# Front of a gated two-branch attention kernel: two loads of weights put first, and a longer slot in the planner of the products

## The chip, the cores and the metric

The kernel runs on one core of a Trainium2 chip. The metric is the device time of one execution in microseconds (us). The kernel is built by a Python program that keeps its own clocks for three engines while it writes out the instructions; these clocks decide the order in which instructions stand, and nothing else. On the chip every engine runs its instructions strictly in that written order and waits where data or buffers are not ready.

## The reference

Two attention branches over the same 2048 rows of 512 numbers are mixed by a gate.

```
qkv = (x @ wqkv).reshape(B, S, 3, H, Dh)        # branch A: 32 heads of 16
idx = pos[:, None] - off[None, :]               # 8 keys per query, 2 apart, going back
logits = einsum("bhsd,bhswd->bhsw", q, kg) * scale
a = (softmax(logits) @ vg) @ wo_a
q = x @ wq; k = x @ wk; v = x @ wv              # branch B: 32 query heads, one key/value head
b = (softmax(q k^T * scale) @ v) @ wo_b
return g * a + (1 - g) * b                      # g = sigmoid((x * gate_w).sum(-1))
```

## The kernel before

The work has four stages on TensorE (PE).

1. **Start** (to 24 us): rows, weights of the query and key are loaded and split into a high part (`xh`, `wqh`, ...) and a low part (`xl`, `wql`, ...); a product in full precision is high x high + high x low + low x high. Keys, and the first two of sixteen query blocks, are made here.
2. **Front** (24 to 278 us, `front_stream`): 14 more query blocks (lumps "q", 2 to 15) and 48 row tiles of branch A's projection (lumps "a": three column groups `gg` = 0, 1, 2 of 16 row tiles each). A lump has 12 products for each half of the contraction rows, all on line L1212. PE can run a product on its upper 64 rows beside one on its lower 64 rows; one such place for two products is a slot. Into the slots are put *max products* of branch B (L382 and L481): scores whose maximum over the keys is wanted before the exponentials start. A lump that is done is copied out of its PSUM bank by ScalarE (ACT): query lumps in two copies, `qraw` (L277) and `qhi` (L278), branch A's in one, `stage` (L315).
3. **Loop** (512 steps, from `exp_pair` and `weighted`): exponentials on ACT (L576), their products with the values on PE (L584), and the max products that the front left over, as pairs into the bank `pm` or as singles into `ps` (L382).
4. **Out phases** (two in the loop, 834 to 901 us and 1196 to 1229 us, L889): output products, with more max products between.

Most max products of the front take a shorter way: for two key blocks the largest of two scores is the half-sum plus the absolute half-difference. A product with the difference key goes to `pm` and ACT takes its absolute value into `dd` (L511); one with the sum key goes to `ps` or `po`, and VectorE (DVE) adds `dd` and takes the maximum (L529). I call the first a difference and the second a sum. PE's next difference into a half of `pm` waits for ACT's L511 of the one before.

Branch A's weights `wa` come in 12 blocks (group `gg`, rows `c` = 0 to 3), each 256 KB. For every block GpSimd (POOL) issues the load into `waraw` (L168, two buffers), ACT makes the high part `wah` (L119), POOL the low part `wal` (L179). `ahead_wa` is called when a lump is done and either loads or splits a block. `load_wa` begins with `settle("low", 0)`: every low part that is planned but not yet written out is written to POOL's queue before the load. So where a block's split is called before the next block's load, the load stands behind that split's low part.

The planner of the front counts a slot as `T_R` = 0.23 us of its own clock `clk["pe"]`; ACT's and DVE's works have planned durations of their own, and a max product is put in when the planned clocks say that its bank is free. The loop and the out phases are planned with the same `T_R`.

Of the kernel before, what the change touches and what calls it, by code (L numbers as in the profile page):

```python
# [19 lines left out]
C = D // P  # L20
# [27 lines left out]
WB = 6  # L48


T_R, T_LAT, T_EXP, T_RED2, T_RED1, T_W, T_TTR = 0.23, 0.20, 0.92, 1.14, 0.61, 1.21, 0.70


class Banks:
# [31 lines left out]
def gated_mix_kernel(ctx, tc, xt, wa, wk, wq, wo_a, wo_b, out):  # L86
# [40 lines left out]
    def after(eng, ready, dur):  # L127
        clk[eng] = max(clk[eng], ready) + dur
        return clk[eng]
# [35 lines left out]
    def load_wa(gg, c):  # L165
        settle("low", 0)
        waraw[gg, c] = p1.tile([P, GN], F32, name="waraw", bufs=2)
        nc.gpsimd.dma_start(waraw[gg, c], wa[c * P:(c + 1) * P, gg * GN:(gg + 1) * GN])  # L168

    def split_wa(gg, c):  # L170
        hi = wah[gg, c] = p1.tile([P, GN], F32R, name="wah", bufs=WB)
        raw = waraw.pop((gg, c))
        high(hi, raw)
        at = after("act", clk["pe"], 0.62)

        def rest():
            nonlocal pool
            wal[gg, c] = p1.tile([P, GN], F32R, name="wal", bufs=WB)
            nc.gpsimd.tensor_sub(wal[gg, c], raw, hi.bitcast(F32))  # L179
            pool = max(pool, clk["pe"] * 1e3) + 1300  # L180

        tasks.append((at + 0.3, rest, (), "low"))

    def ahead_wa(gg, k):

        if 0 <= k < 2 * C and k % 2 == 0:
            load_wa(gg, k // 2)
        if 2 < k <= (2 * C if gg == 0 else 2 * (WB - C)) + 1 and k % 2:
            split_wa(gg, (k - 3) // 2)
# [175 lines left out]
    def fillable():  # L365
        return bool(half) or bool(slots) and slots[0][0] < len(stacked) and stacked[slots[0][0]] <= clk["pe"]
# [85 lines left out]
    def half_keys(g):  # L452

        hb[g] = (m2.shape(2)[:, 0, :], m2[:, 1, :])
        keys = ("m2", "m2")
        clk["pe"] = max(clk["pe"], free["m2"])
        mark("m20", "m21")
        for x in range(2):
            for y in range(2):
                nc.tensor.matmul(hb[g][x], sel[0][:, x * y], kst[:, (2 * g + y) * 512:(2 * g + y + 1) * 512], start=(y == 0), stop=(y == 1))  # L460
        clk["pe"] += 1.2
        for k in keys:
            free[k] = clk["pe"] + 4.0
        tasks.append((clk["pe"] + 1.0, half_parts, (g, keys)))
# [11 lines left out]
    def paired():  # L476
        return len(slots) > 1 and slots[0][3] % 2 == 0 and formed.get(slots[0][3] // 2, 1e9) <= clk["pe"] and slots[1] == slots[0][:3] + (slots[0][3] + 1,) and fillable()
# [7 lines left out]
    def just():  # L485
        return -0.1 if pe else JUST

    def diff_ready(odd):

        if max(half_free) != free["m2"]:  # L490
            half_free[:] = [free["m2"]] * 2
        if half_free[odd] > clk["pe"] - max(0.0, just()) or clk["dve"] - 1.6 > clk["pe"]:
            return False
        mine = [g for g in groups if odd in g[2]]
        if not mine and (groups or half or ended or wants or not paired() or not pe and NF - to_go() >= FRONT):
            return False
        d = mine[0][1] if mine else dd[0]
        return all(x[1] is not d for x in pend[odd])
# [20 lines left out]
    def sum_ready(odd):  # L519

        return bool(pend[odd]) and free[("m1", "po")[odd]] <= clk["pe"] - just() and pend[odd][0][2] <= clk["pe"] + 0.4

    def fill_sum(odd):
        (v, pr, t, kc), d, ready = pend[odd].pop(0)
        m = unit_tile(v)
        dst, key = ((m1, "m1"), (po, "po"))[odd]
        mark(key)
        half_mm(dst, v, pr, t, kc, 0, odd)
        nc.vector.tensor_tensor_reduce(d[:, odd], dst, d[:, odd], 1.0, -FMAX, ALU.add, ALU.max, m[:, odd, pr, t, kc:kc + 1])  # L529
        free[key] = after("dve", max(clk["pe"] + T_R + T_LAT, ready), T_TTR) + 0.08  # L530
        filled(v, 2)
# [35 lines left out]
    pe, pexp, exped = [], {}, {}  # L567
# [482 lines left out]
    def settle(kind, n):  # L1050
        for task in [t for t in tasks if t[3:] == (kind,)][:-n or None]:
            tasks.remove(task)
            task[1](*task[2])
# [169 lines left out]
    def may(b, x, i):  # L1223
        lump = lumps[x]
        if lump[0] == "a" and (lump[1], i // 3) not in wal:
            return False
        return i > 0 or (x - 4 in posted if b == first[x] else x in ends_at and known[0] >= ends_at[x])

    def front_stream():

        n, many = 3 * C, len(lumps)
        lines = [[], []]
        whole_q = [x for x in range(many) if lumps[x][0] == "q"]
        for x in list(range(0, len(whole_q), 4)) + list(range(len(whole_q), many, 4)):
            four = [y for y in range(x, x + 4) if y < many and (lumps[y][0] == lumps[x][0])]
            first.update({y: k % 2 for k, y in enumerate(four)})
            lines[0] += four[0::2] + four[1::2]
            lines[1] += four[1::2] + four[0::2]
        lines = [[(x, i) for x in line for i in range(n)] for line in lines]
        at, idle, begun = [0, 0], 0, False  # L1240
        while min(at) < n * many:
            lone = {}
            if wants and free["m2"] <= clk["pe"] + 0.1:
                half_keys(wants.pop(0))
            halves = groups or any(pend) or paired() and not (half or ended or wants) and free["m2"] <= clk["pe"] + 0.3
            if halves:
                for b in range(2):
                    if sum_ready(b):
                        lone[b] = lambda b=b: fill_sum(b)
                    elif diff_ready(b):  # L1250
                        lone[b] = lambda b=b: fill_diff(b)
                        break
            else:
                for dst, key in ((m1, "m1"), (po, "po")):
                    if not lone and fillable() and free[key] <= clk["pe"] - just():
                        lone[half[0][4] if half else 0] = lambda dst=dst, key=key: fill_one(dst, key)
            moved = []
            for b in sorted((0, 1), key=lambda b: b not in lone):
                if b in lone:
                    now = clk["pe"]  # L1260
                    lone[b]()
                    clk["pe"] = now
                elif at[b] < n * many and may(b, *lines[b][at[b]]):
                    mm(b, lines[b][at[b]])
                    moved.append(lines[b][at[b]])
                    at[b] += 1
            if lone or moved:
                idle = 0
                after("pe", 0, T_R)
            else:  # L1270
                idle += 1
                assert idle < 400
                clk["pe"] += 0.05
                run_tasks()
            if not (ended or wants or halves or formed) and slots and fillable() and free["m2"] <= clk["pe"] - just():
                clk["pe"] = max(clk["pe"], free["m2"])
                fill_pair(m2, "m2")
            for gg in range(1, GG):
                for c in range(WB - C, C):
                    if (gg, c) not in wah and min(at) >= n * (len(whole_q) + gg * NJ - 1) + 3 * (c - WB + C + 1):  # L1280
                        split_wa(gg, c)
            if min(at) >= n * many - 9:
                ended.add(1)
            if min(at) >= n * many - 7 and not begun:
                begun = True
                eb[0] = ebs[0].whole()
                free["e0"] = max(free["f2"], free["f3"])
                exp_pair(0, 0)
            for x, i in moved:
                if i == n - 1 and counted.count(x):  # L1290
                    lump_done(x)
                elif i == n - 1:
                    counted.append(x)
            if moved and moved[-1][1] % 3 == 2:
                run_tasks()
                lump = lumps[min(x for x, i in moved)]
                if p2 and not (lump[0] == "a" and lump[1] + 1 < GG and lump[2] > NJ - 3):
                    run_pool()
# [34 lines left out]
        pool = max(pool, 1e3 * clk["pe"]) + 9000  # L1333

    free.update({f"f{k}": 0.0 for k in range(4)})
    front_stream()
    while groups or any(pend):
        for b in range(2):
# [21 lines left out]
    for s in range(NS + 1):  # L1360
# [17 lines left out]
        k, n = (outs + rows) // 4 - 1, C - (outs >= NJ - 4)  # L1378
# [130 lines left out]
```

## Time and profile before

| | |
|---|---|
| median of 3 runs | 1445.83 us (1444.48 to 1447.59) |
| the profiled execution | 1444.96 us, span 1443.0 us |
| granted TensorE clock | 0.999 |
| PE busy | 1432.9 us, 99% of the span |
| ACT busy | 1297.3 us, 90% |
| DVE busy | 1152.0 us, 80% |
| POOL busy | 963.9 us, 67% |
| front, PE | 2063 products in 254.5 us |

The span runs from the first to the last instruction; the execution's time has 1.96 us around it. A busy PE is no measure here: a product is shown with a modelled length of about 0.39 us while the next one starts 0.11 to 0.23 us after it. What a stretch costs is read from the times at which products start, and from their number in a window.

### The profile page before, as it was taken

What the parts mean: (1) busy time and instruction counts of PE and PEld (TensorE: products, weight loads), DVE (VectorE), ACT (ScalarE), POOL (GpSimd) and SP (SyncE); (2) the same over time, 40 slices, a digit from 0 to 9 for tenths busy, and PEclk for the clock granted to TensorE, in tenths of its full rate; (3) what the DMA queues carried; (4) which work ended last, traced back from release to release, by engine and by line L of the source; (5) the groups of instructions that cost most, each with busy time, mean ns of one, the idle gap of its engine ahead of it and who ended that gap; (6) DMA issues with size and microseconds to landing.
All of it is one profiled execution on the core that took longest, in us unless ns stands there. A gap on an engine that the chain in (4) does not pass through costs nothing.

```text
span 1443.0 us, 29289 instructions
## 1 busy us (share of the span) xinstructions
PE 1432.9 (99%) x10524; PEld 675.9 (47%) x10524; DVE 1152.0 (80%) x1883; ACT 1297.3 (90%) x1649; POOL 963.9 (67%) x1749
## 2 busy tenths in 40 slices
PE   9999999999999999999999999999999999999998
PEld 7877767533333333333333367333333336333343
DVE  8788888788887888888888889788888888788712
ACT  5599888899999999999999988999999998999986
POOL 4541778878898898988988898888888706011220
PEclk9999999999999999999999999999999999999999
DMA  6654533402121110112322210321201011000110
GB/s 228 185 138 111 150 105 91 131 16 87 40 59 48 52 61 2 61 46 68 101 77 67 73 35 31 94 57 42 72 16 69 12 41 35 9 1 2 30 30 30
DMA packets 106969, 94.01 MB, mean 65 GB/s; under 512 B 84880, under 2 KB 89016, under 8 KB 102728
## 3 DMA queue, kind: packets, MB, share of 16 engines
q1 hardware_dynamic: 99864, 52.95, 13.5%
q0 software_dynamic: 6240, 37.89, 8.0%
q8 instruction: 82, 1.34, 0.4%
q10 hardware_dynamic: 720, 1.31, 0.3%
q14 instruction: 63, 0.52, 0.1%
HBM read 62.13 MB, written 29.45 MB: 63 GB/s over the span
## 4 chain that ended last, share of the span: by engine, by line
PE 97%; DMA 1%; ACT 1%; DVE 1%; issue 0%; SPq 0%; POOL 0%; ACTq 0%; POOLq 0%; DVEq 0%
PE po L584 35%; PE pe L574 24%; PE pe L1212 11%; PE pm L382 8%; PE ps L382 5%; PE pe L889 4%; PE pm L481 4%; PE ps L481 2%; PE po L481 2%; PE pm L943 1%; DMA qd<-qhi 0%; ACT pexp L576 0%; PE pe L238 0%; DMA waraw<-wa 0%; PE po L204 0%
## 5 line engine op out<-in xcount | busy, mean ns | idle before, releaser
L576 ACT ACTIVATE pexp<-pe 128x1024 f32<-128x1024 f32 x1022 | 983.2, 1022 | 62.8 <-PE pe L574 60.3
L420 DVE TENSOR_REDUCE mx<-pm 128x2 f32<-128x1024 f32 x486 | 594.9, 1224 | 169.3 <-PE pm L382 162.8
L584 PE MATMUL po<-pexp,vst 128*32 128x512 f32 x4096 | 545.6, 605 | 0.2 <-ACT pexp L576 0.2
L574 PE MATMUL pe<-qst,kst 64*128 64x512 f32 x1788 | 421.7, 455 | 1.7 <-ACT stage L315 0.9
L574 PEld LDWEIGHTS pe<-qst,kst 64*128 64x128 f32 x1788 | 167.6, 183 | 443.7 <-ACT pexp L576 436.6
L432 DVE TENSOR_REDUCE mx<-ps 128x1 f32<-128x512 f32 x303 | 206.2, 681 | 2.6 <-PE ps L382 2.5
L382 PE MATMUL pm<-kst,qst 62*128 62x512 f32 x915 | 186.0, 396 | 0.1
L648 POOL TENSOR_TENSOR pr<-aext 128x256 f32<-128x256 f32 x256 | 181.8, 738 | 4.7 <-DMA aext<-ad 4.5
L711 POOL TENSOR_TENSOR oa<-oa,av 128x256 f32<-128x256 f32 x224 | 164.1, 733 | 15.3
L511 ACT ACTIVATE dd<-pm 128x512 f32<-128x512 f32 x254 | 147.8, 602 | 25.1 <-PE pm L481 5.9
L584 PEld LDWEIGHTS po<-pexp,vst 128*32 128x32 f32 x4096 | 80.7, 108 | 145.2 <-issue 135.8
L708 POOL TENSOR_TENSOR av<-aext,lg 128x256 f32<-128x256 f32 x224 | 139.3, 622 | 12.9
L1212 PE MATMUL pe<-wah,xl 64*128 64x512 f32 x384 | 131.3, 396 | 0.0
L1212 PE MATMUL pe<-wal,xh 64*128 64x512 f32 x384 | 131.0, 395 | 0.0
L1212 PE MATMUL pe<-wah,xh 64*128 64x512 f32 x384 | 129.4, 395 | 0.0
L481 PE MATMUL pm<-kcd,qst 62*128 62x512 f32 x288 | 113.7, 401 | 0.1
L382 PE MATMUL ps<-kst,qst 62*128 62x512 f32 x285 | 112.6, 395 | 0.0
L529 DVE CUSTOM_DVE_ANT_0 dd<-ps,dd 128x512 f32<-128x512 f32 x127 | 87.6, 690 | 17.1 <-PE ps L481 10.1
L529 DVE CUSTOM_DVE_ANT_0 dd<-po,dd 128x512 f32<-128x512 f32 x127 | 87.7, 691 | 11.5 <-PE po L481 7.3
L382 PEld LDWEIGHTS pm<-kst,qst 62*128 62x128 f32 x915 | 88.8, 186 | 2.6 <-DVE mx L420 0.9
L654 POOL TENSOR_TENSOR tr<-pr 128x512 f32<-128x512 f32 x64 | 81.8, 1279 | 4.2
L611 POOL TENSOR_TENSOR rl<-rl,gate_t 128x16 f32<-128x16 f32 x31 | 6.9, 222 | 115.3 <-DVE rl L605 76.0
(205 smaller groups left out, 1997.0 us busy)
## 6 DMA issues: line engine op xcount, KB each, us to landing
aext<-ad POOLq DMA_DIRECT2D x32, 1056.0 KB, 5.5
ad<-stage SPq DMA_DIRECT2D x32, 240.0 KB
qst<-qd SPq DMA_DIRECT2D x56, 128.0 KB
qd<-qhi SPq DMA_DIRECT2D x16, 256.0 KB
qd<-qlo SPq DMA_DIRECT2D x16, 256.0 KB
td<-raw SPq DMA_DIRECT2D x32, 128.0 KB
oa<-td SPq DMA_DIRECT2D x256, 16.0 KB
xraw<-xt SPq DMA_DIRECT2D x15, 256.0 KB
```

The costliest lines, as they stand in the source:

```text
L382: nc.tensor.matmul(dst, qst[home(v)[0]][b:b + 62, pr, t * P:(t + 1) * P], kst[b:b + 62, kc * 512:(kc + 1) * 512], start=True, stop=True)
L420: nc.vector.tensor_reduce(m[:, :, pr, t, kc], dst, AX.X, ALU.max)
L432: nc.vector.tensor_reduce(m[:, odd, pr, t, kc:kc + 1], dst, AX.X, ALU.max)
L481: nc.tensor.matmul(dst, qst[home(v)[0]][b:b + 62, pr, t * P:(t + 1) * P], kcd[b:b + 62, kc // 2, x, :], start=True, stop=True)
L511: nc.scalar.activation(d[:, odd], m2[:, odd, :], AF.Abs)
L529: nc.vector.tensor_tensor_reduce(d[:, odd], dst, d[:, odd], 1.0, -FMAX, ALU.add, ALU.max, m[:, odd, pr, t, kc:kc + 1])
L574: nc.tensor.matmul(bank[:, odd, :], kst[b:b + 64, kt * P:(kt + 1) * P], qst[home(u)[0]][b:b + 64, pr, :], start=True, stop=True)
L576: nc.scalar.activation(e, bank, AF.Exp, scale=SCALE)
L584: nc.tensor.matmul(po[32 * i:32 * i + 32, :], vst[:, kt, :], pexp[s, i // 2][:, i % 2, :], start=(kt == 0), stop=(kt == NJ - 1))
L648: nc.gpsimd.tensor_mul(pr[:, k], q, e[:, o:o + NH, AC:2 * AC])
L711: nc.gpsimd.tensor_add(ao, ao, av)
L1212: nc.tensor.matmul(front_bank(x), l[h], r[h], start=(not second and i == 0), stop=(second and i == 3 * C - 1))
```

## The change

Two things are done.

- Before the front begins, the loads of group 0's blocks 0 and 1 are issued; `ahead_wa` no longer issues these two. All other blocks are loaded where `ahead_wa` says.
- The front's planner counts a slot in which something was placed as `T_F` = 0.235 us, in place of `T_R` = 0.23. `T_R` stays everywhere else.

```diff
-T_R, T_LAT, T_EXP, T_RED2, T_RED1, T_W, T_TTR = 0.23, 0.20, 0.92, 1.14, 0.61, 1.21, 0.70
+T_F, T_R, T_LAT, T_EXP, T_RED2, T_RED1, T_W, T_TTR = 0.235, 0.23, 0.20, 0.92, 1.14, 0.61, 1.21, 0.70
...
     def ahead_wa(gg, k):

-        if 0 <= k < 2 * C and k % 2 == 0:
+        if (4 if gg == 0 else 0) <= k < 2 * C and k % 2 == 0:
             load_wa(gg, k // 2)
         if 2 < k <= (2 * C if gg == 0 else 2 * (WB - C)) + 1 and k % 2:
             split_wa(gg, (k - 3) // 2)
...
             if lone or moved:
                 idle = 0
-                after("pe", 0, T_R)
+                after("pe", 0, T_F)
...
     free.update({f"f{k}": 0.0 for k in range(4)})
+    for c in range(2):
+        load_wa(0, c)
     front_stream()
```

The first part alone leaves the order on PE as it was. The second moves the order of nearly the whole program. In numbers of instructions: PE's front has 2070 products where it had 2061 (4 differences and 5 sums more), and 1476 products' worth of maxima are left for the loop where 1484 were. The first out phase has 151 max products beside its 384 output products, where it had 164; the second 75 beside 192, where it had 84. The loop's three stretches (before, between and after the out phases) have 150, 95 and 49 singles, where they had 156, 84 and 45, and 542, 284 and 127 products in pairs, where they had 542, 284 and 123.

The order of two neighbouring lumps also turns: where lump 10 was done before lump 11, and row tile 4 before tile 5, the odd one is now done first. An even lump is the one that loads a block, an odd one the one that splits.

Three places show what this does. In the rows the first name is what is written, the number behind a name tells buffers of one name apart.

POOL, group 0's blocks 0 and 1, before: from the load of block 0 to the load of block 1.

```order
L168 DMA waraw_505<-wa 128x512
L283 TENSOR_TENSOR qlo_502<-qraw_500,qhi_501 128x512
L283 TENSOR_TENSOR qlo_516<-qraw_514,qhi_515 128x512
L283 TENSOR_TENSOR qlo_647<-qraw_645,qhi_646 128x512
L179 TENSOR_TENSOR wal_666<-waraw_505,wah_650 128x512
L168 DMA waraw_668<-wa 128x512
```

The same place now, behind the last low part of the rows.

```order
L123 TENSOR_TENSOR xl_117<-xraw_129,xh_112 128x512
L168 DMA waraw_336<-wa 128x512
L168 DMA waraw_338<-wa 128x512
L283 TENSOR_TENSOR qlo_454<-qraw_452,qhi_453 128x512
L283 TENSOR_TENSOR qlo_462<-qraw_460,qhi_461 128x512
```

The load of block 1 stood behind the low part of block 0 and now stands ahead of all query lumps.

POOL, group 0's blocks 2 (`waraw_733`) and 3, before.

```order
L179 TENSOR_TENSOR wal_731<-waraw_668,wah_716 128x512
L168 DMA waraw_733<-wa 128x512
L283 TENSOR_TENSOR qlo_728<-qraw_726,qhi_727 128x512
L168 DMA waraw_854<-wa 128x512
L283 TENSOR_TENSOR qlo_851<-qraw_849,qhi_850 128x512
L283 TENSOR_TENSOR qlo_863<-qraw_861,qhi_862 128x512
L179 TENSOR_TENSOR wal_907<-waraw_733,wah_866 128x512
```

The same place now.

```order
L179 TENSOR_TENSOR wal_731<-waraw_338,wah_716 128x512
L168 DMA waraw_733<-wa 128x512
L283 TENSOR_TENSOR qlo_726<-qraw_724,qhi_725 128x512
L283 TENSOR_TENSOR qlo_854<-qraw_852,qhi_853 128x512
L179 TENSOR_TENSOR wal_867<-waraw_733,wah_857 128x512
L168 DMA waraw_869<-wa 128x512
```

The load of block 3 stood two rows behind the load of block 2; now the low parts of query lump 11 (`qlo_854`) and of block 2 stand ahead of it.

POOL, group 1's blocks 0 (`waraw_1245`, `waraw_1259` now) and 1, before.

```order
L168 DMA waraw_1245<-wa 128x512
L168 DMA waraw_1405<-wa 128x512
L546 TENSOR_TENSOR mt_1327<-mt_1327,mk_75 128x32
L547 TENSOR_TENSOR ml_1381<-mt_1327,mh_1379 128x32
L179 TENSOR_TENSOR wal_1455<-waraw_1245,wah_1420 128x512
L168 DMA waraw_1466<-wa 128x512
L179 TENSOR_TENSOR wal_1523<-waraw_1405,wah_1481 128x512
```

The same place now.

```order
L168 DMA waraw_1259<-wa 128x512
L546 TENSOR_TENSOR mt_1317<-mt_1317,mk_75 128x32
L547 TENSOR_TENSOR ml_1369<-mt_1317,mh_1367 128x32
L179 TENSOR_TENSOR wal_1432<-waraw_1259,wah_1423 128x512
L168 DMA waraw_1434<-wa 128x512
L179 TENSOR_TENSOR wal_1490<-waraw_1434,wah_1486 128x512
```

The load of block 1 stood right behind that of block 0, ahead of every split; it now stands between the low parts of blocks 0 and 1.

ACT at that place, now: from the high part of block 0 to that of block 1.

```order
L119 ACTIVATE wah_1423<-waraw_1259 128x512
L511 ACTIVATE dd_572<-pm_748 128x512
L315 ACTIVATE stage_1430<-pe0_89 128x512
L511 ACTIVATE dd_573<-pm_747 128x512
L339 ACTIVATE gate_t_74<-gate_73 32x16
L511 ACTIVATE dd_573<-pm_748 128x512
L511 ACTIVATE dd_572<-pm_747 128x512
L315 ACTIVATE stage_1484<-pe1_95 128x512
L119 ACTIVATE wah_1486<-waraw_1434 128x512
L315 ACTIVATE stage_1488<-pe1_94 128x512
```

Before, eight rows lay between these two high parts (four L511, two L315, two L339); now seven, with one L339 less.

Group 2 has the same turn. On POOL the load of its block 1 stood ahead of the low part of block 0, with three rows between; it now stands right behind that low part, and ahead of that low part there is now one of four multiplications of L648 where four stood. On ACT seven rows (four L511, two L315, one of L376) lie between the high parts of its blocks 0 and 1, where five lay (three L511, two L315).

## The prediction

> **What bounds the kernel now.** I read the page's chain by engine, then the windows of the front and of the two out phases, then who waits for the blocks of `wa`, and last the chain inside the loop.
>
> ```profile
> PE 97%; DMA 1%; ACT 1%; DVE 1%; issue 0%; SPq 0%; POOL 0%; ACTq 0%; POOLq 0%; DVEq 0%
> ```
>
> ```profile
> core 0: us, PE busy (x) PEld busy (x) DVE busy (x) ACT busy (x) POOL busy (x), PEclk, DMA share, GB/s
> 24.10:278.60 254.50, 252.22 (x2063) 190.60 (x2062) 218.39 (x589) 206.18 (x420) 152.30 (x249) 1.00 0.45 125
> 100.00:180.00 80.00, 80.00 (x684) 60.69 (x682) 70.39 (x210) 72.60 (x145) 33.58 (x56) 1.00 0.46 127
> 180.00:278.60 98.60, 98.38 (x786) 68.25 (x782) 84.99 (x254) 82.17 (x155) 79.72 (x156) 1.00 0.35 99
> 834.30:900.90 66.60, 66.60 (x553) 49.33 (x549) 58.33 (x171) 55.11 (x99) 58.31 (x100) 1.00 0.09 32
> 1196.30:1229.30 33.00, 33.00 (x280) 24.70 (x278) 29.97 (x88) 28.45 (x50) 23.61 (x40) 1.00 0.09 31
> ...
> 70.00:278.00 208.00, 207.70 (x1710) 151.16 (x1708) 178.72 (x531) 181.88 (x355) 130.40 (x229) 1.00 0.42 118
> ```
>
> The chain runs through PE, at a full clock, so a change is worth what it does to PE's order of starts. In the windows the reader divides time by the number of PE's products: 254.5 / 2063 = 0.1234 us each over the whole front, 0.1170 between 100 and 180 us, 0.1254 after that, and 66.6 / 553 = 0.1204 and 33.0 / 280 = 0.1179 in the out phases. ACT is busy for 72.6 of 80 us in the middle of the front and DVE for 70.4: three engines in lockstep, none with much to spare.
>
> ```profile
> PEld pm L481 <- ACT dd L511: 17.7, 67, 0.5
> ```
>
> This is who waits in the front: PE's weight loads for differences stand 67 times behind ACT's absolute values. So when ACT stops, PE soon stops.
>
> **The wait that the early loads take away.** ACT, then POOL, then PE in the same microseconds:
>
> ```profile
> 50.07 0.63 ACT L119 ACTIVATE wah<-waraw 128x512 fp32r<-128x512 f32 x1
> ...
> 53.65 0.59 ACT L278 ACTIVATE qhi<-pe 128x512 fp32r<-128x512 f32 x1
> 57.13 0.63 ACT L119 ACTIVATE wah<-waraw 128x512 fp32r<-128x512 f32 x1 [2.89 <-DMA waraw<-wa]
> ```
> ```profile
> 51.43 1.29 POOL L179 TENSOR_TENSOR wal<-waraw,wah 128x512 fp32r<-128x512 f32 x1
> 52.66 0.56 POOL L168 DMA_DIRECT2D waraw<-wa  x1
> ```
> ```profile
> 56.56 0.39 PE L1212 MATMUL pe<-xh,wql 64*128 64x512 f32 x1
> 58.79 0.50 PE L1212 MATMUL pe<-xh,wqh 64*128 64x512 f32 x1 [1.83 <-ACT qhi L278]
> ```
>
> The low part of block 0 stands ahead of block 1's load on POOL, so the load cannot go out until ACT has made block 0's high part. From the start of that high part (call it W, 50.07) it is 52.66 - 50.07 = 2.59 us to the load's issue and 57.13 - 50.07 = 7.06 us to block 1's high part. ACT stood idle for 2.89 us of these, the copies of a query lump behind it, and PE had to wait for that lump's bank: 58.79 - 56.56 = 2.23 us between two starts where a slot takes 0.23,
>
> ```profile
> 65.34 0.40 PE L1212 MATMUL pe<-xl,wqh 64*128 64x512 f32 x1
> ...
> 67.18 0.61 PE L1212 MATMUL pe<-xl,wqh 64*128 64x512 f32 x2
> ```
>
> (eight slots in 1.84 us), so PE lost 2.0 us: 0.69 of ACT's wait. The loads now go out where POOL has ended the rows' low parts:
>
> ```profile
> 23.44 5.52 POOL L123 TENSOR_TENSOR xl<-xraw,xh 128x512 fp32r<-128x512 f32 x4 [9.61 <-ACT xh L119]
> 36.28 1.29 POOL L283 TENSOR_TENSOR qlo<-qraw,qhi 128x512 fp32r<-128x512 f32 x1 [7.32 <-DVE mx L432]
> ```
>
> That is 28.96 us, 20 us ahead of the first split; the two issues, 0.56 us each, lie in the 7.32 us in which POOL idles, and without that cover they would cost POOL 1.1 us for which nobody waits yet. **Term 1: -2.0 us.**
>
> **The waits that the turned order makes.** The same pattern, low part then load then the next high part, now stands in three other places: group 0's blocks 2 and 3, blocks 0 and 1 of groups 1 and 2. Before, none of these high parts waited:
>
> ```profile
> 69.14 0.65 ACT L119 ACTIVATE wah<-waraw 128x512 fp32r<-128x512 f32 x1
> ...
> 72.67 0.67 ACT L119 ACTIVATE wah<-waraw 128x512 fp32r<-128x512 f32 x1
> ...
> 108.38 0.64 ACT L119 ACTIVATE wah<-waraw 128x512 fp32r<-128x512 f32 x1
> ...
> 112.86 0.63 ACT L119 ACTIVATE wah<-waraw 128x512 fp32r<-128x512 f32 x1
> ...
> 173.03 0.66 ACT L119 ACTIVATE wah<-waraw 128x512 fp32r<-128x512 f32 x1
> ...
> 176.56 0.65 ACT L119 ACTIVATE wah<-waraw 128x512 fp32r<-128x512 f32 x1
> ```
> ```profile
> 109.10 1.30 POOL L179 TENSOR_TENSOR wal<-waraw,wah 128x512 fp32r<-128x512 f32 x1 [2.45 <-ACT wah L119]
> 110.69 0.58 POOL L168 DMA_DIRECT2D waraw<-wa  x1 [0.30 <-POOL wal L179]
> ...
> 176.02 1.28 POOL L179 TENSOR_TENSOR wal<-waraw,wah 128x512 fp32r<-128x512 f32 x1
> 177.60 0.58 POOL L168 DMA_DIRECT2D waraw<-wa  x1 [0.30 <-POOL wal L179]
> ```
> ```profile
> DMA to landing us min/median/max: 3.1/4.3/6.3
> ...
> DMA to landing us min/median/max: 3.1/3.2/3.4
> ```
>
> The first of the last two rows is of all twelve loads, the second of those between 158 and 192 us. Each time I take W as the first high part's start, and compare when the next block lands with when ACT would come to it.
>
> - Group 1: the pattern stands in the trace with another block behind it. Issue at W + 2.31 (110.69 - 108.38), landing 4.3 later: W + 6.6. ACT comes to it at W + 4.48 by the rows before, a quarter microsecond sooner with one small row less between: it waits 2.4 us.
> - Group 0: query lump 11's low part (1.29 us, as other POOL rows of 512 columns) comes first, then the low part, so about W + 3.1 and landing at W + 7.4. ACT needed 72.67 - 69.14 = 3.53 us before; three more rows of about 0.5 us stand between now (a lump's two copies and one L511): W + 5.0. It waits 2.4 us.
> - Group 2: POOL came to the low part 2.99 us after W, since four multiplications stood ahead; one does now, so the issue lies between W + 2.3 and W + 4.57, and 3.2 later, as loads take there, the landing between W + 5.5 and W + 7.8. ACT had 3.53 us and has one L511 and one small row more: about W + 4.2. It waits 1.3 to 3.6 us; I take the middle, 2.4.
>
> Behind the waiting high part stand a lump's copy and the next absolute values; for these PE's differences wait (the 67 waits above) and for PE's sums DVE. By the measured 0.69, 3 x 2.4 x 0.69 = 5.0. **Term 2: +5.0 us.** Below: with the shortest landing, 3.1, ACT waits 5.4 - 4.5 = 0.9 us, and just that much (2.89 - 2.0) was absorbed once, so 0. Above: the pattern that was measured, 7.06, against 4.2, and nothing absorbed, 3 x 2.9 = 8.7. The middle is taken because the one measured case lies there.
>
> The Trainium skill, "DMA: Bandwidth & Descriptors", section "Anatomy of one DMA — SWDGE (gpsimd) path", speaks against this term: it gives a load issued by GpSimd about 2.0 us and its bytes at 436 GB/s, which would be an estimated 2.6 us for 256 KB, a landing at W + 4.9 and hardly a wait. The trace has no load of this tile under 3.1 us, so I stay with the rows; the sum by the page would be that of the second rival below.
>
> **More products in the front.** Nine more, at the front's mean of 0.1234 us, which has its usual waits in it: **term 3: +1.1 us.** Above: if a sum's round through PE, ACT and DVE sets the pace, five sums more at 208 us / 253 = 0.82 us (70 to 278 us, where the order has 253 of them) are 4.1. Below: nothing is bought, since a product takes a place on PE; whether the longer slot removes waits is the third rival.
>
> **Loop and out phases.** The chain in the loop:
>
> ```profile
> 283.64 1.00 PE po L584 x8
> ...
> 285.06 0.24 PE pm L382 x2
> 285.30 0.23 PE ps L382
> 285.53 0.23 PE pe L574 x2
> 285.76 1.00 PE po L584 x8
> ...
> 287.18 0.23 PE pm L382 x2
> 287.41 0.24 PE pe L574 x2
> ```
>
> A step with a single (`ps`) is 285.76 - 283.64 = 2.12 us, one without ends at 287.65: 1.89. A single costs 0.23 us, and so does a pair. Nine more singles (150 + 95 + 49 against 156 + 84 + 45) and two more pairs: 11 x 0.23 = +2.5. The out phases have 13 and 9 products less: 13 x 0.1204 + 9 x 0.1179 = -2.6. **Term 4: -0.1 us**, at nothing; if the singles fell where ACT holds the step anyway it would be -2.6, if the out phases are held by ACT and DVE +2.5.
>
> **The sum**: -2.0 + 5.0 + 1.1 - 0.1 = +4.0 us. The profiled execution took 1444.96 us (its span 1443.0 and 1.96 around it), 0.87 below the median of 1445.83. On the one scale this gives 1449.0, on the other 1449.8; I say 1449.4. I take 0.2%, 2.9 us, as what a measurement here can tell from no change.
>
> **Rivals.**
>
> *The new waits reach PE* (the forecast): 1446.5 to 1453, chance 0.46; of these 0.08 lie within 0.2%.
>
> *They don't*: the loads land in 3.1 us or ACT has work to spare. For it: the loads after 158 us land in 3.1 to 3.4 us, and 0.9 us was absorbed once. Against: the median, and ACT's 72.6 of 80 us. Then -2.0 + 0 + 1.1 - 0.1 = -1.0 and 1444.4, no change. This is where the skill's 2.6 us would lead. Chance 0.28.
>
> *The front loses its waits* (faster): the longer slot brings each product to its bank when it is free. The 1710 products between 70 and 278 us would run at the clean 0.115 us: 196.7 in place of 208, -11.3 us, and the sum would be -7.3: 1438. It decides from 6.9 us of these 11.3 on. Against: the order goes the other way, with more differences and sums among the same 1488 products of L1212, so each stands fewer slots behind the one that it waits for. Chance 0.14.
>
> *The waits come in full and the sums set the pace* (far slower): ACT's 7.2 us unabsorbed and 4.1 for five sums: -2.0 + 7.2 + 4.1 - 0.1 = +9.2, 1454.6. For it: DVE's and ACT's shares in the middle of the front. Chance 0.12.
>
> So slower has 0.38 + 0.12 = 0.50, the same 0.28 + 0.08 = 0.36, faster 0.14. The range 1444.0 to 1454.5 leaves out the third rival and a third of the fourth, 0.18.
>
> **What would show it.** Right: no wait of ACT on block 1 at 57 us, and three on later blocks, 2 to 3 us each; the front's PE ends 4 us later than before, the first out phase takes 1.6 us less and the second 1.1. Wrong: fewer than two waits of ACT on `waraw`, or waits that leave PE's pitch at 0.117 through 100 to 180 us; or a front that ends before 278 us.

## The result and the profile after

The changed kernel takes 1456.18 us (median of 6 executions, 1454.45 to 1460.40); the kernel before took 1446.44 beside it (6 executions, 1444.48 to 1447.59). The ratio is 1.0072, 95% interval [1.0056, 1.0088]: slower by 0.7%, 9.7 us between the medians. The forecast was 1449.4 us, slower by 4 us; its range ended at 1454.5. The profiled execution took 1456.70 us, span 1454.9, granted clock 0.997.

First the chain by engine and the windows of PE's stages (columns as in the prediction). The last four rows are two stretches of 3.4 us and what follows each.

```profile
PE 93%; DMA 2%; POOL 2%; ACT 1%; DVE 1%; issue 1%; SPq 0%; ACTq 0%; POOLq 0%; DVEq 0%
```
```profile
core 0: us, PE busy (x) PEld busy (x) DVE busy (x) ACT busy (x) POOL busy (x), PEclk, DMA share, GB/s
23.70:291.30 267.60, 258.45 (x2071) 192.98 (x2070) 222.65 (x599) 209.38 (x425) 153.23 (x251) 0.99 0.43 119
100.00:180.00 80.00, 77.89 (x656) 57.33 (x654) 68.85 (x203) 70.33 (x139) 26.19 (x46) 1.00 0.42 119
180.00:291.30 111.30, 106.33 (x838) 74.54 (x834) 90.18 (x270) 88.25 (x168) 88.55 (x169) 0.98 0.36 96
845.60:910.70 65.10, 65.10 (x548) 48.82 (x541) 56.81 (x159) 51.22 (x91) 56.65 (x97) 1.00 0.09 33
1206.50:1239.80 33.30, 33.30 (x277) 24.44 (x269) 29.29 (x78) 25.43 (x45) 23.38 (x40) 1.00 0.10 32
...
74.70:78.10 3.40, 3.40 (x17) 2.92 (x17) 2.38 (x9) 2.30 (x6) 2.33 (x2) 0.50 0.79 220
78.10:116.00 37.90, 37.72 (x316) 27.84 (x314) 32.77 (x97) 33.40 (x70) 13.42 (x17) 1.00 0.38 104
187.30:190.70 3.40, 3.37 (x16) 2.69 (x18) 1.00 (x3) 1.84 (x5) 3.22 (x6) 0.50 0.51 121
190.70:250.00 59.30, 59.25 (x488) 42.95 (x486) 51.96 (x155) 50.15 (x95) 48.68 (x95) 1.00 0.35 98
```

Four per cent of the chain has gone from PE: two to POOL, one to DMA and one to issue. The front now lasts 267.6 us for 2071 products; before, 254.5 for 2063. Taken from start to start of its products, it grew from 253.98 to 267.03 us, by 13.05, and began 0.46 earlier; the rest of the kernel became 0.7 us shorter. So the loss is the front's. In two stretches of 3.4 us the granted clock is 0.50, which no stretch of the front showed before.

Who waits, from 24 to 290 us (who, for whom, us in total, times, the longest):

```profile
PEld pm L481 <- ACT dd L511: 28.5, 72, 4.3
...
PE pm L481 <- ACT dd L511: 8.2, 7, 3.9
ACT wah L119 <- DMA waraw<-wa: 6.7, 2, 4.2
ACT qraw L277 <- POOL qlo L283: 2.6, 2, 1.9
```

Before, no wait in the first of these groups was longer than 0.5 us; now there are some of 2 to 4.3. ACT waits twice for a block of `wa`, and for a query lump's low part. The next fences show the three places on ACT, POOL and PE.

```profile
66.19 0.63 ACT L119 ACTIVATE wah<-waraw 128x512 fp32r<-128x512 f32 x1
...
70.79 0.60 ACT L277 ACTIVATE qraw<-pe 128x512 f32<-128x512 f32 x1 [1.92 <-POOL qlo L283]
...
73.19 0.66 ACT L119 ACTIVATE wah<-waraw 128x512 fp32r<-128x512 f32 x1
...
111.15 0.63 ACT L119 ACTIVATE wah<-waraw 128x512 fp32r<-128x512 f32 x1
...
117.60 0.63 ACT L119 ACTIVATE wah<-waraw 128x512 fp32r<-128x512 f32 x1 [2.49 <-DMA waraw<-wa]
...
177.85 0.64 ACT L119 ACTIVATE wah<-waraw 128x512 fp32r<-128x512 f32 x1
...
186.16 0.63 ACT L119 ACTIVATE wah<-waraw 128x512 fp32r<-128x512 f32 x1 [4.16 <-DMA waraw<-wa]
```
```profile
67.64 1.30 POOL L179 TENSOR_TENSOR wal<-waraw,wah 128x512 fp32r<-128x512 f32 x1
68.87 0.55 POOL L168 DMA_DIRECT2D waraw<-wa  x1
69.44 1.31 POOL L283 TENSOR_TENSOR qlo<-qraw,qhi 128x512 fp32r<-128x512 f32 x1
...
113.10 0.58 POOL L168 DMA_DIRECT2D waraw<-wa  x1
...
177.55 1.28 POOL L654 TENSOR_TENSOR tr<-pr 128x512 f32<-128x512 f32 x1
...
180.74 0.75 POOL L648 TENSOR_TENSOR pr<-aext 128x256 f32<-128x256 f32 x1
181.45 1.30 POOL L179 TENSOR_TENSOR wal<-waraw,wah 128x512 fp32r<-128x512 f32 x1
182.68 0.58 POOL L168 DMA_DIRECT2D waraw<-wa  x1
```
```profile
72.42 0.50 PE L481 MATMUL pm<-kcd,qst 62*128 62x512 f32 x1 [1.56 <-ACT dd L511]
...
119.25 0.50 PE L481 MATMUL pm<-kcd,qst 62*128 62x512 f32 x1 [2.02 <-ACT dd L511]
...
187.33 0.79 PE L481 MATMUL pm<-kcd,qst 62*128 62x512 f32 x1 [3.88 <-ACT dd L511]
...
187.92 0.62 PE L1212 MATMUL pe<-wah,xl 64*128 64x512 f32 x2
188.35 0.63 PE L1212 MATMUL pe<-wah,xh 64*128 64x512 f32 x2
```

- Group 1: with W = 111.15, block 1's load goes out at W + 1.95 and block 1 is split at W + 6.45. ACT waited 2.49 us. PE's starts are 2.42 us apart there, 2.19 more than a slot.
- Group 2: W = 177.85. POOL, busy with branch A's rows of L648 to L674, came to the low part 3.60 us later and to the load at W + 4.83; the block was split at W + 8.31. ACT waited 4.16 us and PE lost 4.05 (4.28 between starts).
- Group 0: ACT doesn't wait for block 3's load. But block 2's low part and that load stand ahead of lump 10's low part on POOL, and the copy of lump 12 (`qraw`, the same buffer as lump 10's) waits for the latter: 1.92 us on ACT, 1.95 between PE's starts, 1.72 lost. The load took 3.9 us and landed at about 72.8 us, W + 6.6 (W = 66.19); ACT comes to it at 73.19. Without the 1.92 us ACT would have been there at about W + 5.1, by estimate, and would have waited 1.5 us. So the load was in time only because ACT had been held already.
- After 187.33 slots begin 0.43 us apart (187.92, 188.35) where 0.23 is usual: that is the half clock of the windows.

The wait of 2.89 us on group 0's block 1, shown before, is gone.

### The profile page after: what moved, and what is told of

Same layout as the page of the kernel before. It is cut to its first block, busy times and chain, and to the rows that moved or that the text cites. A ratio compares the mean times of both kernels' runs of the same rounds, so it can differ in the third digit from the quotient of the medians.

```text
span 1454.9 us, 29251 instructions
## 1 busy us (share of the span) xinstructions
PE 1437.8 (99%) x10524; PEld 677.1 (47%) x10524; DVE 1157.4 (80%) x1877; ACT 1291.7 (89%) x1637; POOL 966.1 (66%) x1753
## 4 chain that ended last, share of the span: by engine, by line
PE 93%; DMA 2%; POOL 2%; ACT 1%; DVE 1%; issue 1%; SPq 0%; ACTq 0%; POOLq 0%; DVEq 0%
PE po L584 35%; PE pe L574 24%; PE pe L1212 9%; PE pm L382 8%; PE ps L382 5%; PE pe L889 4%; PE pm L481 3%; PE ps L481 2%; PE po L481 1%; PE pm L943 1%; POOL pr L648 1%; DMA waraw<-wa 1%; ACT dd L511 0%; DMA aext<-ad 0%; DMA qd<-qhi 0%
## 5 line engine op out<-in xcount | busy, mean ns | idle before, releaser
L420 DVE TENSOR_REDUCE mx<-pm 128x2 f32<-128x1024 f32 x492 | 602.0, 1223 | 168.0 <-PE pm L382 161.5
L432 DVE TENSOR_REDUCE mx<-ps 128x1 f32<-128x512 f32 x315 | 214.3, 680 | 1.7 <-PE ps L382 1.7
L648 POOL TENSOR_TENSOR pr<-aext 128x256 f32<-128x256 f32 x256 | 181.8, 737 | 6.1 <-DMA aext<-ad 5.8
L511 ACT ACTIVATE dd<-pm 128x512 f32<-128x512 f32 x258 | 150.1, 603 | 28.7 <-PE pm L481 8.5
L382 PE MATMUL ps<-kst,qst 62*128 62x512 f32 x301 | 119.0, 395 | 0.0
L481 PE MATMUL pm<-kcd,qst 62*128 62x512 f32 x272 | 110.0, 407 | 7.6 <-ACT dd L511 7.5
L529 DVE CUSTOM_DVE_ANT_0 dd<-po,dd 128x512 f32<-128x512 f32 x129 | 89.1, 691 | 19.9 <-PE po L481 11.9
```

What stands on the lines that cost most here:

```text
L382: nc.tensor.matmul(dst, qst[home(v)[0]][b:b + 62, pr, t * P:(t + 1) * P], kst[b:b + 62, kc * 512:(kc + 1) * 512], start=True, stop=True)
L420: nc.vector.tensor_reduce(m[:, :, pr, t, kc], dst, AX.X, ALU.max)
L432: nc.vector.tensor_reduce(m[:, odd, pr, t, kc:kc + 1], dst, AX.X, ALU.max)
L481: nc.tensor.matmul(dst, qst[home(v)[0]][b:b + 62, pr, t * P:(t + 1) * P], kcd[b:b + 62, kc // 2, x, :], start=True, stop=True)
L511: nc.scalar.activation(d[:, odd], m2[:, odd, :], AF.Abs)
L648: nc.gpsimd.tensor_mul(pr[:, k], q, e[:, o:o + NH, AC:2 * AC])
```

## The experiments

Twelve kernels ran, 5 to 11 executions each. All carry the early loads except where said. The median stands with the ratio to the kernel before and its interval; the front is PE's time from its first to its last start in the profiled execution (before 253.98 us, after 267.03).

| kernel | median us | ratio | front us |
|---|---|---|---|
| `loads_only` | 1442.60 | 0.9981 [0.9972, 0.9990] | 252.01 |
| `slot_only` | 1456.72 | 1.0077 [1.0063, 1.0091] | 265.80 |
| `loads_turned` | 1444.81 | 0.9998 [0.9989, 1.0007] | 254.42 |
| `turned_low2` | 1447.77 | 1.0014 [1.0005, 1.0023] | 255.56 |
| `turned_low4` | 1452.11 | 1.0044 [1.0030, 1.0057] | 260.66 |
| `after_sp` | 1447.42 | 1.0016 [1.0007, 1.0024] | 257.62 |
| `after_fill` | 1454.35 | 1.0061 [1.0048, 1.0075] | 264.92 |
| `after_sp_q` | 1447.50 | 1.0013 [1.0004, 1.0022] | 256.65 |
| `after_early` | 1455.99 | 1.0065 [1.0053, 1.0078] | 261.57 |
| `early_225` | 1445.58 | 1.0004 [0.9995, 1.0012] | 253.42 |
| `sp_225` | 1449.39 | 1.0026 [1.0016, 1.0037] | 255.54 |
| `sp_240` | 1455.58 | 1.0072 [1.0060, 1.0085] | 268.18 |

**Each half alone.** `loads_only` takes the slot back:

```diff
-T_F, T_R, ... = 0.235, 0.23, ...
+T_F, T_R, ... = 0.23, 0.23, ...
```

> Only the early loads, the planner's slot back at 0.23. Waits theory (the added time is ACT standing before blocks that land late, handed on to PE): block 1's wait at 57 us is gone and no other comes, PE gains 2.0 us: 1.4 to 2.6 us under the kernel before, ratio 0.9986. Slot theory (the longer slot itself makes the front slower, whatever waits): the same here, or nothing if the 2.0 us are taken back by the lockstep of the three engines.

The front is 1.97 us shorter with PE's order unchanged, and no wait of ACT on `waraw` is left. The early loads are worth 2 us of front. By the medians this version lies 3.2 us under the kernel before beside it (1445.82), by the ratio 2.7 with an interval of 1.4 to 4.1; it is faster than both kernels.

`slot_only` keeps 0.235 and loads blocks 0 and 1 as before (`ahead_wa` with its old condition, no early loads).

> Only the longer slot, the loads of group 0's blocks 0 and 1 where the planner puts them. The order on PE is that of the changed kernel, and on POOL both loads now stand ahead of the first low part. If the loads' early place is worth nothing once the order has turned: like the changed kernel within 1.5 us, about 1456. If it is worth the 2.0 us of the wait before: 1458.

It is as slow as the changed kernel, with the same PE order and gaps of 1.89, 1.92 and 3.99 us at the same three places. Under that order block 1's load already goes out ahead of block 0's split (POOL issues it at 47.41 us, ACT splits block 0 at 51.53), so the early loads have nothing to remove. The change's loss is that of the slot alone.

**The waits taken away.** `after_sp` lets SP issue the three loads in question, so that they stand behind nothing on POOL; PE's order is that of the changed kernel.

```diff
-        nc.gpsimd.dma_start(waraw[gg, c], wa[c * P:(c + 1) * P, gg * GN:(gg + 1) * GN])
+        eng = nc.sync if (gg, c) in ((0, 3), (1, 1), (2, 1)) else nc.gpsimd
+        eng.dma_start(waraw[gg, c], wa[c * P:(c + 1) * P, gg * GN:(gg + 1) * GN])
```

> The changed kernel with three loads (group 0's block 3, block 1 of groups 1 and 2) issued by SP in place of POOL, so that they need not stand behind a low part; PE's order is exactly that of the changed kernel. Waits theory: the two waits of 2.49 and 4.16 us on ACT go, and the halved clock behind the second; the wait in group 0 (ACT behind a query lump's low part on POOL) loses 0.5 us: 7 to 9 us under the changed kernel, about 1448. Slot theory: 1455, and the front still ends past 288 us.

No ACT wait on `waraw` is left, the gaps at 119 and 187 us are gone, group 0's shrank from 1.95 to 1.39 us (the issue is off POOL, the low part is not), and no stretch of the front is at half clock. SP issues the two blocks 1 at 102.0 and 168.0 us, where POOL came to them at 113.1 and 182.7: 11 and 15 us sooner, far more than the 2.9 to 4.7 us in which a load of the changed kernel lands. So it is the place that matters there, and not a quicker load. The front, and its middle, in its windows:

```profile
core 0: us, PE busy (x) PEld busy (x) DVE busy (x) ACT busy (x) POOL busy (x), PEclk, DMA share, GB/s
23.50:281.60 258.10, 255.44 (x2071) 189.03 (x2070) 222.34 (x599) 209.10 (x424) 151.69 (x247) 1.00 0.44 123
100.00:180.00 80.00, 79.91 (x676) 59.27 (x674) 70.41 (x209) 72.68 (x144) 30.73 (x53) 1.00 0.44 127
```

Between 100 and 180 us PE starts 676 products, where the changed kernel starts 656. So the place of the loads on POOL's queue costs 8.8 us by the medians (8.1 when each median is set against the kernel before beside it), 9.4 in the front. The two gaps account for 6.24 of the 9.4 (2.19 + 4.05) and group 0 for 0.56; 2.6 us are over.

**The waits made in the old order, and doubled.** `loads_turned` keeps the slot at 0.23 and before's PE order, and only loads block 1 of groups 1 and 2 after block 0's split.

```diff
-        if (4 if gg == 0 else 0) <= k < 2 * C and k % 2 == 0:
+        if 4 <= k < 2 * C and k % 2 == 0 or gg and k == 0:
...
+            if gg and k == 3:
+                load_wa(gg, 1)
```

> Slot 0.23 and early loads, PE's order exactly that of the kernel before; the one edit is that block 1 of groups 1 and 2 is loaded behind block 0's split, as the longer slot made it. Waits theory: PE stands still 2.2 us near 115 us and 4 us near 180 us, and the clock halves for 3.4 us after the longer one: 6 to 8 us over loads_only, about 1451. Slot theory: at most 1.5 us over loads_only.

The waits came, but smaller than I had said: 1.00 and 1.88 us on ACT. In group 2 POOL had no rows of branch A ahead here; in group 1 the load took 3.5 us to land, where it took 4.5 in the changed kernel, and ACT came to it 0.5 us later. It is 2.2 us of time over `loads_only` in place of 6 to 8. The two next kernels write block (1,0)'s low part two and four times.

```diff
-            nc.gpsimd.tensor_sub(wal[gg, c], raw, hi.bitcast(F32))
+            for _ in range(2 if (gg, c) == (1, 0) else 1):
+                nc.gpsimd.tensor_sub(wal[gg, c], raw, hi.bitcast(F32))
```

> Like loads_turned, but the low part of block (1,0) is written twice on POOL, so block (1,1)'s load goes out 1.29 us later and nothing else moves on PE. Passed-through theory: ACT's wait at block (1,1) grows from 1.0 to 2.3 us, PE's gap at 113 us from 0.86 to about 2.1, no clock drop, and the time is 1.2 us above loads_turned (about 1446.0). Rival, that ACT's wait is absorbed by work in hand: the gap stays under 1.2 and the time within 0.3 us.

> The same with the low part of block (1,0) written four times: 3.87 us later. Passed-through theory with a clock drop: ACT waits 4.9 us, PE's gap at 113 us is 4.5 to 4.8 us, the granted clock falls to half for about 3.4 us behind it, which costs another 1.3 to 1.7 us, and the time is 5 to 6 us above loads_turned (about 1450). Without a clock drop it is 3.9 above (1448.7). Absorbed (0.69 and less of the wait): 2.7 or less above (1447.5).

ACT's waits on `waraw` and PE's next difference, first in `turned_low2`, then in `turned_low4`:

```profile
ACT wah L119 <- DMA waraw<-wa: 3.9, 2, 2.1
```
```profile
113.60 0.49 PE L484 MATMUL pm<-kcd,qst 62*128 62x512 f32 x1 [1.57 <-ACT dd L514]
```
```profile
ACT wah L119 <- DMA waraw<-wa: 6.9, 2, 4.9
```
```profile
111.57 0.39 PE L1215 MATMUL pe<-wah,xh 64*128 64x512 f32 x1
116.31 0.79 PE L484 MATMUL pm<-kcd,qst 62*128 62x512 f32 x1 [4.36 <-ACT dd L514]
```

With the two cases of the changed kernel this gives a row of ACT's wait against what PE lost (start to start, less a slot of 0.23): 1.00 and 0.63, 1.88 and 1.39, 2.1 and 1.74, 2.49 and 2.19, 4.16 and 4.05, 4.9 and 4.51. It is the wait less 0.1 to 0.5 us, not a fixed share of it. Two other cases lie outside: the wait of 2.89 us before the change cost 2.0, where PE stood behind a query lump's copies and not behind a difference, and one of 1.73 us in `sp_240`, below, cost 2.28. In `turned_low4`'s profiled execution the clock is 0.50 for 6.8 us, from 114.9 to 121.7 us, and its front is 6.24 us longer than that of `loads_turned`, where the gap grew by 3.88. Its median is 7.3 us above that of `loads_turned`, where I had said 5 to 6.

The medians differ by more than the fronts. The executions of `turned_low2` say why, by their mean granted clock: four at 1.000 took 1445.6 to 1446.6 us, three at 0.999 1447.8 to 1448.6, two at 0.998 1447.3 and 1449.7, two at 0.997 1450.1 and 1450.3. The same kernel loses some of the clock in some executions and not in others; I had expected none. A mean of 0.999 can also come from the end of the span alone: in the profiled execution of the kernel before the clock is 0.50 only in the last 2.3 us, when PE has ended. Without the loss, the second writing of the low part costs 1.1 us (1445.9 against 1444.8, the medians of the executions at 1.000), as forecast for a wait that is passed on.

**The clock drop by itself.** `after_fill` is the changed kernel with PE kept at work in the long gaps of groups 0 and 2 by products of zeros, added into banks that are being filled.

```diff
+        upto[b] = (x, i, r)
+        count[0] += 1
+        for k in range(FILL.get(count[0], 0)):
+            y, j, to = upto[k % 2]
...
+            h = slice(64 * (k % 2), 64 * (k % 2) + 64)
+            nc.tensor.matmul(front_bank(y), zeros_r[h], to[h], start=False, stop=False)
...
+    count, upto, FILL = [0], {}, {303: 10, 927: 28}
```

> The changed kernel, whose PE order, loads and waits all stay, with 38 products of zeros (10 ahead of the difference that starts at 72.4 us, 28 ahead of the one at 187.3), added into banks that are being filled, so that PE works through the two long waits where it stood idle; the outputs don't change. At 0.115 us each they need 1.15 of the 1.95 us and 3.2 of the 4.3. If the idle stretches are what makes the granted clock fall to half behind them, the drops at 74.7 and 187.3 us go and the time falls by 1.3 to 1.7 us for each: 1452.5 to 1454 against 1456.2. If the drops have nothing to do with PE's idleness, they stay, and the time is that of after or above it by what the products cost (0 to 1 us).

The windows of the 3.4 us behind the two filled gaps:

```profile
core 0: us, PE busy (x) PEld busy (x) DVE busy (x) ACT busy (x) POOL busy (x), PEclk, DMA share, GB/s
72.90:76.30 3.40, 3.31 (x20) 2.08 (x22) 2.16 (x8) 3.30 (x8) 2.21 (x3) 1.00 0.82 234
187.30:190.70 3.40, 3.36 (x28) 2.70 (x30) 2.25 (x8) 2.95 (x7) 3.22 (x6) 1.00 0.47 113
```

```profile
185.49 0.39 PE L1224 MATMUL pe<-wal,zeros_r 64*128 64x512 f32 x1
187.34 0.50 PE L483 MATMUL pm<-kcd,qst 62*128 62x512 f32 x1 [1.47 <-ACT dd L513]
```

The difference still starts at 187.34 us, so the wait is still there; but 28 products start in the next 3.4 us at a clock of 1.00, where the changed kernel started 16 at 0.50. Twelve products at 3.4 / 28 = 0.121 us are 1.5 us. The same products can also be timed in several traces. The 15 that start from 74.68 us on take 3.38 us in the changed kernel and 2.22 in both `after_fill` and `after_sp`; the 16 from 187.33 us on take 3.51, 1.96 and 1.84. So the two stretches at half clock cost 1.2 and about 1.6 us, and these are the 2.6 us that were over. All five timed executions show a clock of 1.000 (the changed kernel: 0.994 to 0.998), and the median is 1.8 us lower (1.4 against the kernel before beside each, and a little above the 1452.5 to 1454 that I had said); the front is 2.1 shorter although ACT waited 7.3 us on `waraw` here, 0.6 more. An idle PE is what costs the clock. That is shown for these two places together; it was not tried at the gap of group 1, where no drop was seen.

**What is left without the waits.** `after_sp` is still 4.8 us slower than `loads_only`. `after_sp_q` also writes group 0's block 2 low part behind lumps 10 and 11 on POOL.

```diff
-        settle("low", 0)
+        settle("low", int((gg, c) == (0, 3)))
...
-        tasks.append((at + 0.3, rest, (), "low"))
+        tasks.append((at + (2.6 if (gg, c) == (0, 2) else 0.3), rest, (), "low"))
```

> after_sp (SP issues the three loads; PE order of after), and besides, group 0's block 2 gets its low part on POOL after the low parts of lumps 10 and 11 instead of ahead of them; PE's, ACT's and DVE's order stay. If the copy of lump 12 waits at 70 us because lump 10's low part stands behind that block on POOL, the 1.36 us of ACT's wait go, PE's gap at 71.6 us shrinks from 1.39 to under 0.6, and the time is 0.9 to 1.3 us below after_sp: 1446.1 to 1446.5. If the wait has another end behind it, the gap stays over 1 us and the time within 0.4 us of 1447.4.

The gap at 71.6 us is gone (nothing over 0.49 us there) and the front 0.97 us shorter, as said; the medians, 1447.50 and 1447.42, don't show it. Among the executions at a clock of 1.000 the difference is 0.6 us (1446.7 against 1447.3), but `after_sp_q` has five of eleven at 0.998 and `after_sp` three. So the mechanism of group 0 holds in the trace, and its worth in time is too small for these runs. 4.6 us of front remain against `loads_only`: nine products more, 1.1 us, and 3.5 spread over it.

Is that the slot's length? `after_early` (0.235) and `early_225` (0.225) load blocks 0 and 1 of groups 1 and 2 together on POOL, and a load there no longer has the low part of the block before it written ahead of it; `sp_225` and `sp_240` are `after_sp` with other slots.

```diff
-        settle("low", 0)
+        settle("low", int((gg, c - 1) in wah and (gg, c - 1) not in wal))
...
+        if gg and k == 0:
+            load_wa(gg, 0)
+            load_wa(gg, 1)
-        if (4 if gg == 0 else 0) <= k < 2 * C and k % 2 == 0:
+        if 4 <= k < 2 * C and k % 2 == 0:
```

> The changed kernel with its slot of 0.235, but blocks 0 and 1 of groups 1 and 2 are both loaded at the group's start, so that the load of block 1 no longer stands behind block 0's low part on POOL. If the long waits and the clock drops behind them are what the change costs, the gaps at 119 and 187 us go and the time is that of after_sp or a little above, 1447 to 1449.5. If the longer slot itself costs it, it stays at 1454 to 1457.

> after_early with a slot of 0.225 instead of 0.235: the order turns the other way round, with fewer products in the front. If a longer slot costs by its length (the rest of about 5 us between loads_only and after_sp is spread over the front), this is 4 us or more below after_early, and at or below loads_only (1442.6). If the rest belongs to the one place in group 0 where a lump's copy waits for POOL, it is within 1 us of loads_only or above it.

> The early loads, the three later loads on SP as in after_sp, and a slot of 0.225. What is left between loads_only (0.23, 1442.6) and after_sp (0.235, 1447.4) is 4.8 us. If the length of the slot costs it (1 us for each 0.001), this is at or below loads_only: 1438 to 1443. If each order has its own small waits and 0.23 happens to be a good one, this is above loads_only too: 1444 to 1447.

> The same with a slot of 0.240. If the length of the slot costs 1 us for each 0.001, this is 1451 to 1453; if the orders differ without a trend, 1444 to 1449.

`after_early` missed: it has no wait on `waraw`, and its front is 5.5 us shorter than that of the changed kernel, but from group 2 on its order is another one. A gap of 1.84 us still stands at 186.7 us, now behind DVE. Its first out phase takes 69.64 us for 548 products where that of `loads_only` takes 66.29 for as many, and the clock is 0.50 for 6.8 us from 74.3 us, after group 0's gap, and for 3.4 us from 289.3. Its one execution at a mean clock of 1.000 took 1452.2 us, the others, at 0.996 to 0.998, 1455.7 to 1456.7. It settles nothing on the slot.

With the loads on SP the slots 0.225, 0.235 and 0.240 give 1449.4, 1447.4 and 1455.6 us; 0.230 without a wait, 1442.6. There is no slope of 1 us for each 0.001: a shorter slot is slower too, and `sp_225` and `sp_240` are both slower than either theory said. `sp_225`, `sp_240` and `early_225` all have a new wait in group 0, where ACT waits 2.1, 1.7 and 1.7 us for a block and PE's starts are 2.07, 2.51 and 1.66 us apart; behind it the clock is 0.50 for 3.4 us, from 73.8, 77.0 and 73.6 us. `early_225`, with the same slot as `sp_225` and other places of the loads (and, with them, an order that differs in places), is 3.8 us faster and 3 us above `loads_only`. That is where its second theory put it, but by another wait of group 0 than the one that this theory names. No run has a slot of 0.23 with loads on SP, so what SP's issuing itself may cost is not separated from the slot. Here are the rows of `sp_240` and of `early_225`:

```profile
75.35 0.49 PE L482 MATMUL pm<-kcd,qst 62*128 62x512 f32 x1 [2.12 <-ACT dd L512]
```
```profile
71.29 0.49 PE L484 MATMUL pm<-kcd,qst 62*128 62x512 f32 x1 [1.27 <-ACT dd L514]
```

So what a slot costs depends, in these runs, on which works it brings together around 70 us and in the groups. The spread 3.5 us between `loads_only` and `after_sp_q` I could not put down to single waits.

## Why the prediction was wrong

The direction was right, and the mechanism too at two of the three places; the size was not: 4.0 us forecast, 9.7 by the medians, 11.9 between the profiled spans (the profiled execution of the kernel before lies 1.5 us under its median here, that of the changed kernel 0.5 over).

- **Term 1** (-2.0) held: `loads_only` measured -1.97 us of front. But with the longer slot alone that wait is gone already, so the hoist adds nothing to this change.
- **Term 2** (+5.0) is the step that failed. Two waits stood where I put them, and a third at the place but with another cause; PE lost 2.19 + 4.05 + 1.72 = 8.0 us. Three things were mis-sized. The share of 0.69, from one case in which 0.9 us were absorbed, is not a share: of ACT's waits of 1.92, 2.49 and 4.16 us, 0.90, 0.88 and 0.97 came through. Group 2's load went out at W + 4.83 and landed at W + 8.3, where I gave at most W + 4.57 and W + 7.8, because I counted the multiplications of L648 that stood ahead on POOL and not the whole run of branch A's rows. And in group 0 ACT didn't wait for the load, but I had not counted who stood behind it on POOL: lump 10's low part, for which lump 12's copy waits.
- **What term 2 lacked** is the clock: two stretches of 3.4 us at half speed behind the gaps, 1.8 us by the median of `after_fill`, 2.7 by the same products in the traces. In the trace of before the one long gap, 2.22 us at 58.8 us, had cost no clock, and I took a gap to cost its own length.
- **Term 3** (+1.1) was too small. Without the long waits, the longer slot costs 5.6 us of front (252.01 to 257.62): 1.0 is group 0's wait, by `after_sp_q`, and 4.6 stay, a little over the upper end of 4.1. That the sums set the pace, which gave this upper end, is not shown: 3.5 of the 4.6 have no cause here.
- **Term 4** (-0.1) held: the first out phase became 2.36 us shorter (1.6 said), the second 0.54 (1.1), the three parts of the loop together 2.2 longer (2.5 said), -0.7 in all.

In fronts of profiled executions the way from before over `loads_only` and `after_sp` to the changed kernel is -1.97 for the early loads, +5.61 for the slot without the long waits and +9.41 for the waits and the clock, 13.05 in all. These are differences along one chain, so that they add up is no test.

Of the rivals, "they don't reach PE" fell with ACT's waits of 2.49 and 4.16 us. "The front loses its waits" fell: PE's waits on `dd` rose from 17.7 us in 67 to 28.5 in 72. "The waits come in full and the sums set the pace" was nearest: its 7.2 us of waits measured 8.0 and its 4.1 measured 4.6 to 5.6; it had no term for the clock. That its +9.2 lies so near the 9.7 of the medians is in part luck, since it leaves the clock out and the profiled spans differ by 11.9. I gave it 0.12, because the only wait in the trace had been absorbed in part; that one case carried too much.

## What to carry to other kernels

A load that is issued by an engine that also computes is in a queue: count everything ahead of it, and everything that it and its forerunner push back. Where PE waits for ACT within a slot or two, a wait of 2 us or more can be passed on almost in full (here 1.4 to 4.5 us of waits of 1.9 to 4.9) and can cost the clock besides; the one wait of 2.89 us of which 0.69 was passed on said little about the others. A planner's constant that sets an order is not a knob with a slope; change it, and read off which loads, low parts and copies have changed places, and where one can, make those places safe first.

## What the hardware showed that I had not expected

In the profiled executions the granted clock fell to 0.50 for 3.4 us at a time, twice for 6.8, when PE had stood idle (a drop): at the end of a gap of 4.28 us, within one of 4.74, behind one of 1.95 us that was followed by 2.3 us with 13 products in them, and behind one of 1.66 us in `early_225`. After gaps of 2.42 us (the changed kernel, group 1), 2.22 (before) and 1.97 (`turned_low2`) the profiled executions show none. So the length of a gap doesn't decide it. A drop can also come in one execution of a kernel and not in the next. The executions of `early_225` fall in two groups: six at a mean clock of 1.000 took 1444.9 to 1445.6 us, five at 0.999, the profiled one with its one drop among them, 1446.7 to 1447.5.

The clock records of the traces say more. The drops of one execution start a whole number of steps of 3.413 us apart: 74.68 and 187.32 us in the changed kernel are 33 steps, and `slot_only`, `after_early` and `sp_240` have 33 and 31, 63, and 64. If the time from 24 to 330 us is cut into these steps in all 14 profiled executions, 28 products start in a usual step at full clock. All eight full-clock steps with at most 11 products were followed by half clock; of those with 12 to 14, four were and eleven were not (the step of the 2.42 us gap has 12); none with more was.

The Trainium skill, "TensorE: Matmul & The Clock Gate", section "What's actually happening", describes a clock of two states that is set by a free-running window of about 3.4 us. The traces agree on the two states (1.00 and 0.50), on the 3.4 us and on a grid that the gaps don't move; no run here moved one gap against that grid on purpose, so whether the place alone decides stays open. In the Trainium skill the same page's section "HAM oscillation — how this bites in real kernels" puts the danger at idle gaps above 3.4 us; here a gap of 1.95 us with thin work behind it was enough.
